# Attention in front of two dense blocks: the causal mask of the first two row tiles moves from TensorE to VectorE, one of six copies moves from ScalarE to VectorE, and the steps of a pair are written in another order

## The chip, the cores and the metric

The kernel runs on one core of a Trainium2 chip. Its time is the device time of one launch in microseconds (us), the median of several runs. TensorE (PE in the profile, PEld for its weight loads), VectorE (DVE), ScalarE (ACT) and GpSimd (POOL) each work through their own instructions in the order in which the program gives them; SyncE (SP) issues the transfers. An engine waits for another only through semaphores.

## The reference

Attention over 2 x 12 heads with 448 positions and a head size of 64, causal, in float32; then two dense blocks.

```python
scores = scale * np.matmul(q, k.transpose(0, 1, 3, 2))
mask = np.triu(np.ones((seq, seq), dtype=bool), k=1)
scores = np.where(mask, -1000000000.0, scores)
scores = scores - np.max(scores, axis=-1, keepdims=True)
attn = np.exp(scores)
attn = attn / (np.sum(attn, axis=-1, keepdims=True) + 1e-09)
attn_out = np.matmul(attn, v)
...
h = np.maximum(np.maximum(x @ w1, x @ w2), x @ w3)
x = h @ w_out
...
h = x @ w_in
r = np.maximum(h, 0.0)
out = (s * (r * r) + b) @ moe2_w_out
```

Here x has 896 rows and 768 columns.

## The kernel before

**Tiles.** Two heads make a pair; there are 12 pairs. The 448 positions of a head are four row tiles of 112, called 0 to 3, and row tile i needs the scores of the first 112 (i + 1) columns alone. `scores` (line 278) multiplies q and k for one or two row tiles of both heads into a PSUM tile `s`: six products of split operands for a row tile (line 296), the two heads in the upper and the lower half of TensorE's rows. After them come four small products of `eye` and `mask` (line 303), each 112 columns wide, which add a large negative number above the diagonal. VectorE takes the negated row maxima `mx` out of PSUM (line 312), ScalarE the exponentials into `P` with the row sums `su` (line 320). `transpose_p` (line 355) turns the 20 blocks of 112 x 112 of a pair on TensorE, in six PSUM tiles `t` (A for the first head, B for the second; 0, 1 and 2 for the column blocks 0, 1 and 2 with 3), which are copied to `PT` (line 474). `pv` (line 372) multiplies `PT` with v into the PSUM tile `o`.

**The sums.** VectorE adds 1e-9 to `su` and takes the reciprocal (steps N1 and N2, lines 478 and 481). TensorE transposes the 8 columns (RT), VectorE copies them out (RV, line 340), SyncE stores them (Q1) and spreads them over all partitions into `rb` (Q2). VectorE multiplies `o` with `rb` (XM, line 398), and GpSimd makes two parts of the result (XO, XL).

**The order.** `emit(p)` builds a table of steps by name and issues them in the order of the list `ORDER`, once for each pair; for the last two rounds, 12 and 13, by the lists in `ORDER_END`. A round p works on three pairs at once: scores, maxima and exponentials of pair p (Sb, Rb, Eb: row tile 2; Sc, Rc, Ec: row tile 3) and of pair p + 1 (Sa, Ra: row tiles 1 and 0; their exponentials Ea come in the next round), the transposes of pair p - 1 (TA0 to TB2, copies VA0 to VB2) and the products with v of pair p - 2 (P0 to P3). LD, QS, HS and LS load, scale and split q and k of later pairs: HS on VectorE, QS and LS on GpSimd. W1, W2, W3 and Y belong to the decoding of the dense blocks' weights and do something from round 10 on. `keep_busy` (line 435) issues filler products in the first rounds. There are two PSUM tiles for scores, three for transposes and one for `o`, so Sc(p) waits until Ea(p) has read Sa(p)'s tile, Sa(p + 1) until Eb(p) has read Sb(p)'s, and each group of transposes until the copy three groups before it is done.

**The dense blocks** (line 559 on) follow the last round. They are the same in both kernels.

Of the kernel before, what the change touches and what calls it, by code (L numbers as in the profile page):

```python
# [8 lines left out]
F32 = mybir.dt.float32  # L9
# [6 lines left out]
ALU = mybir.AluOpType  # L16
# [8 lines left out]


ORDER = (
    "N1 N2 TA0 Q2 LD Ea TA1 QS VA0 Sb TA2 VA1 VA2 Rb W1 HS TB0 TB1 RT Eb RV Q1 Y TB2 Sc Sa "
    "P0 Rc HS0 VB0 VB1 Ra Y VB2 P1 P2 P3 LS XM XO XL Ec"
).split()  # L30

ORDER_END = (
    "TA0 VA0 TA1 VA1 TA2 VA2 Q2 N1 N2 TB0 VB0 TB1 RT VB1 RV Q1 TB2 VB2 W1 P0 P1 P2 P3 Y Y "
    "XM XO XL W2 Y Y".split(),
    "P0 P1 P2 P3 Q2 W1 M1 M2 Y Y W2 XM XO XL M3 M4 Y Y W3 Y Y".split(),
)
# [5 lines left out]
MASKED = -(2.0 ** 30)  # L42
# [11 lines left out]
def kernel(  # L54
# [14 lines left out]
    nc = tc.nc  # L69
# [149 lines left out]
    def attention():  # L219
        with ExitStack() as c2:  # L220
            pool = lambda n, b, **kw: c2.enter_context(tc.tile_pool(name=n, bufs=b, **kw))
            mk = pool("mk", 1)
            mask, eye = (mk.tile([128, 2, CH], BF16, name=n) for n in ("mask", "eye"))
            ld = pool("ld", 4)
            vp = pool("vp", 6)
            ap = pool("ap", 3)
# [51 lines left out]
            def scores(p, tiles):  # L278

                e = pair[p]
                if "P" not in e:
                    e["P"] = p_p.tile([CH, 2, PW], F32, tag="P", name="P")
                    e["mx"] = sm.tile([CH, NC, 2], F32, tag="mx", name="mx")
                    e["su"] = sm.tile([CH, 2 * NC], F32, tag="su", name="su")
                ps = ps_s.tile([128, 2, 512], F32, tag="s", name="s")[0:CH]
                hl = [e["HL"][h * D:(h + 1) * D] for h in range(2)]
                o = 0
                offs = []  # L290
                for i in tiles:
                    n = (i + 1) * CH
                    qs = slice(i * CH, n)
                    for m, (a, c) in enumerate(((0, 2), (1, 2), (0, 3))):
                        for h in range(2):
                            nc.tensor.matmul(  # L296
                                ps[:, h, o:o + n], hl[h][:, a, qs], hl[h][:, c, 0:n],
                                start=(m == 0), stop=False, skip_group_check=True,
                            )
                    for m in range(2):  # L300
                        for h in range(2):
                            rows = slice(h * D, (h + 1) * D)
                            nc.tensor.matmul(  # L303
                                ps[:, h, o + n - CH:o + n], eye[rows, m], mask[rows, m],
                                start=False, stop=(m == 1), skip_group_check=True,
                            )
                    offs.append((i, o, n))
                    o += n

                def maxima():  # L310
                    for i, o, n in offs:
                        nc.vector.tensor_reduce(  # L312
                            out=e["mx"][:, i], in_=ps[:, :, o:o + n], op=ALU.max,
                            axis=mybir.AxisListType.X, negate=True,
                        )

                def exponentials():
                    for i, o, n in offs:
                        for h in range(2):
                            nc.scalar.activation(  # L320
                                out=e["P"][:, h, poff[i]:poff[i] + n], in_=ps[:, h, o:o + n],
                                func=ACTF.Exp, bias=e["mx"][:, i, h:h + 1], scale=1.0,
                                accum_out=e["su"][:, h * NC + i:h * NC + i + 1],
                            )

                return maxima, exponentials

            def weights_out(p, ps):

                e = pair[p]  # L330
                ps = ps[0:2 * NC, 3 * CH:4 * CH]
                rows = n_p.tile([2 * NC, CH], F32, tag="rows", name="rows")
                dram = dr_p.tile([2 * NC, CH], F32, tag="rcd", name="rcd")
                e["rb"] = n_p.tile([128, S], F32, tag="rb", name="rb")

                def transpose():
                    nc.tensor.transpose(ps, e["su"], ident[0:CH, 0:CH])  # L337

                def evacuate():
                    nc.vector.tensor_copy(out=rows, in_=ps)  # L340

                def store():
                    nc.sync.dma_start(out=dram, in_=rows)

                def spread():
                    src = dram.rearrange("(h i) n -> h (i n)", h=2)
                    for h in range(2):
                        nc.sync.dma_start(
                            out=e["rb"][h * D:(h + 1) * D],
                            in_=src[h:h + 1].to_broadcast([D, S]),  # L350
                        )

                return transpose, evacuate, store, spread
# [83 lines left out]
                    nc.tensor.matmul(ps, ones[:, 0:128], ones, start=True, stop=True)  # L437

            keep_busy(WARM)
            split_first(0)  # L440

            first = early_products(ps_s, "s")
# [2 lines left out]
            def emit(p):  # L445
                ops = {}
                if 0 <= p < n_pairs:
                    for n in "bc":
                        ops["S" + n] = lambda n=n: score[p].update(
                            {n: scores(p, (2,) if n == "b" else (3,))}  # L450
                        )
                        ops["R" + n] = lambda n=n: score[p][n][0]()
                    for n in "abc":
                        ops["E" + n] = lambda n=n: score[p][n][1]()
                    if p + 3 < n_pairs:
                        ops["LD"] = lambda: load(p + 3)
                    if p + 2 < n_pairs:
                        ops["QS"] = lambda: scale_q(p + 2)
                        ops["HS" if p else "HS0"] = lambda: split_hi(p + 2)
                        ops["LS"] = lambda: split_lo(p + 2, nc.gpsimd)  # L460
                if p + 1 < n_pairs:
                    ops["Sa"] = lambda: score[p + 1].update(a=scores(p + 1, (1, 0)))
                    ops["Ra"] = lambda: score[p + 1]["a"][0]()
                if 0 <= p - 1 < n_pairs:
                    d = {}
                    for h, k in enumerate("AB"):
                        for n, js in (("0", (0,)), ("1", (1,)), ("2", (2, 3))):
                            ops["T" + k + n] = lambda n=k + n, h=h, js=js: d.update(
                                {n: transpose_p(p - 1, h, js)}
                            )  # L470
                            copy = nc.scalar.copy
                            if p == n_pairs and n == "1":
                                copy = nc.vector.tensor_copy
                            ops["V" + k + n] = lambda n=k + n, copy=copy: copy(  # L474
                                out=d[n][0], in_=d[n][1]
                            )
                    su = pair[p - 1]["su"]
                    ops["N1"] = lambda: nc.vector.tensor_scalar(
                        out=su, in0=su, scalar1=1e-9, scalar2=None, op0=ALU.add
                    )  # L480
                    ops["N2"] = lambda: nc.vector.reciprocal(out=su, in_=su)

                    def rt():
                        pair[p - 1]["r"] = r = weights_out(p - 1, d["B1"][2])
                        r[0]()

                    ops["RT"] = rt
                    ops["RV"] = lambda: pair[p - 1]["r"][1]()
                    ops["Q1"] = lambda: pair[p - 1]["r"][2]()
                if 0 <= p - 2 < n_pairs:  # L490
                    ops["Q2"] = lambda: pair[p - 2]["r"][3]()
                    for j in range(NC):
                        ops[f"P{j}"] = lambda j=j: pv(p - 2, (j,))
                    for n, fn in zip(("XM", "XO", "XL"), pv_out(p - 2)):
                        ops[n] = fn
                if p == n_pairs + 1:
                    ops.update({f"M{n}": lambda: next(first) for n in (1, 2, 3, 4)})
                for n in CHUNKS.get(p, "").split():
                    ops[n] = begin
                ops["Y"] = lambda: finish(1)  # L500
                for n in ORDER if p < n_pairs else ORDER_END[p - n_pairs]:
                    if n in ops:
                        ops[n]()
                    if (p, n) in WARM_AT:
                        keep_busy(WARM_AT[p, n])
# [211 lines left out]
```

## Time and profile before

| what | value |
|---|---|
| median of 3 runs | 509.93 us (509.84 to 510.24) |
| the profiled execution's own time | 510.31 us |
| its span, first to last instruction | 508.5 us |
| TensorE busy over the span | 500.2 us (98%) |
| VectorE, ScalarE, GpSimd busy | 331.5, 307.1, 230.1 us |
| mean granted TensorE clock | 0.999 of full speed |

Attention takes the first 95 us of the span, the dense blocks the rest. A busy share counts the time that an engine's records cover. TensorE's records overlap, since it takes up the next product before the last has drained, so what a group of products costs is read from its own start to the start of the next group, not from the length of its records.

### The profile page before, as it was taken

How to read it: one execution, taken by the hardware profiler on the slowest of the kernel's cores; microseconds unless marked ns; L12 is line 12 of the kernel's file. 1: busy time of each engine (PE TensorE's matmuls, PEld its weight loads, DVE VectorE, ACT ScalarE, POOL GpSimd, SP SyncE). 2: the span in 40 equal slices, each digit the busy share in tenths (PEclk: the TensorE clock that was granted, in tenths of full speed). 3: DMA queues.
4: the chain of work that ended last, by engine and by line, in shares of the span. 5: the costliest groups of instructions: out<-in, count | busy, mean ns of one | idle time of the engine just before them, and what ended most of it. 6: DMA issues, size and time to landing. Idle time of an engine off the chain costs nothing.

```text
span 508.5 us, 8350 instructions
## 1 busy us (share of the span) xinstructions
PE 500.2 (98%) x3060; PEld 453.1 (89%) x3062; DVE 331.5 (65%) x642; ACT 307.1 (60%) x740; POOL 230.1 (45%) x216
## 2 busy tenths in 40 slices
PE   8899999999999999999999999999999999999997
PEld 4677777789999999999999999999999999999996
DVE  4666667787665756666666666767777985387601
ACT  4899999645453544635444888888888542354201
POOL 4556663435353443434323566666656543134300
PEclk9999999999999999999999999999999999999999
DMA  8343343433343323323332333233323352244003
GB/s 230 115 146 121 115 132 111 136 96 118 124 125 119 113 78 126 100 92 120 125 123 73 115 124 110 81 121 124 96 91 126 125 177 91 109 169 172 15 1 108
DMA packets 16185, 58.39 MB, mean 115 GB/s; under 512 B 2384, under 2 KB 6224, under 8 KB 16144
## 3 DMA queue, kind: packets, MB, share of 16 engines
q1 hardware_dynamic: 16144, 57.85, 34.5%
q8 instruction: 24, 0.39, 0.3%
q14 instruction: 17, 0.14, 0.1%
HBM read 55.05 MB, written 2.80 MB: 114 GB/s over the span
## 4 chain that ended last, share of the span: by engine, by line
PE 94%; ACT 2%; DMA 1%; DVE 1%; issue 0%; SPq 0%; POOL 0%; ACTq 0%; POOLq 0%
PE m L526 57%; PE m L647 23%; PE o L383 4%; PE t L364 4%; PE s L296 4%; ACT P L320 1%; DMA R<-in_qk_dram 1%; PE s L303 1%; PE o L526 1%; DVE mx L312 1%; ACT PT L474 0%; PE warm L437 0%; SPq L245 0%; PE t L337 0%; DVE HL L258 0%
## 5 line engine op out<-in xcount | busy, mean ns | idle before, releaser
L526 PE MATMUL m<-x,whi 128*128 128x448 f32 x804 | 228.4, 365 | 0.6 <-ACT t L535 0.6
L188 POOL TENSOR_TENSOR wa<-wa,wr 128x384 int32<-128x384 int32 x112 | 130.0, 1161 | 207.9 <-DVE wa L180 171.5
L526 PEld LDWEIGHTS m<-x,whi 128*128 128x128 f32 x804 | 150.8, 188 | 13.0 <-ACT t L535 1.0
L526 PE MATMUL m<-x,wlo 128*128 128x448 f32 x402 | 146.8, 365 | 0.0
L169 DVE TENSOR_SCALAR wa<-wa 128x384 f32<-128x384 f32 x112 | 74.4, 664 | 77.9 <-ACT wa L168 77.6
L647 PE MATMUL m<-whi,g 128*128 128x384 f32 x448 | 114.0, 334 | 0.0
L199 ACT CAST whi<-wa 128x384 fp32r<-128x384 f32 x111 | 56.4, 509 | 64.9 <-PE m L647 32.8
L647 PEld LDWEIGHTS m<-whi,g 128*128 128x128 f32 x448 | 81.0, 188 | 0.0
L526 PEld LDWEIGHTS m<-x,wlo 128*128 128x128 f32 x402 | 75.5, 188 | 6.0
L647 PE MATMUL m<-wlo,g 128*128 128x384 f32 x224 | 74.8, 334 | 0.0
L101 DVE TENSOR_TENSOR wlo<-wa,whi 128x384 fp32r<-128x384 f32 x112 | 62.2, 557 | 13.7 <-ACT whi L199 13.6
L180 DVE SCALAR_TENSOR_TENSOR wa<-wraw,wa 128x384 int32<-128x384 int32 x112 | 62.5, 558 | 3.8
L161 ACT ACTIVATE wr<-wraw 128x384 int32<-128x384 uint32 x112 | 61.5, 549 | 0.3 <-DMA wraw<-in_w_dram 0.2
L168 ACT ACTIVATE wa<-wraw 128x384 f32<-128x384 f32 x110 | 59.6, 541 | 0.0
L320 ACT ACTIVATE P<-s,mx 112x224 f32<-112x224 f32 (+3 forms) x96 | 46.3, 498 | 9.0 <-DVE mx L312 7.8
L174 DVE TENSOR_SCALAR wa<-wa 128x384 int32<-128x384 int32 x112 | 43.6, 390 | 3.8
L647 PEld LDWEIGHTS m<-wlo,g 128*128 128x128 f32 x224 | 42.0, 188 | 0.0
L526 PE MATMUL m<-h,whi 128*128 128x448 f32 x144 | 40.9, 365 | 0.0
L312 DVE TENSOR_REDUCE mx<-s 112x2 f32<-112x448 f32 (+3 forms) x48 | 33.5, 735 | 9.8 <-PE s L303 9.2
L101 POOL TENSOR_TENSOR g<-r,g 128x448 fp32r<-128x448 f32 x32 | 37.2, 1162 | 0.0
L364 PE MATMUL t<-ident,P 112*112 112x112 f32 x240 | 29.8, 264 | 1.5 <-ACT PT L474 1.5
L474 ACT COPY PT<-t 112x336 f32<-112x336 f32 (+1 forms) x70 | 29.8, 497 | 1.9 <-PE t L364 0.8
(64 smaller groups left out, 471.7 us busy)
## 6 DMA issues: line engine op xcount, KB each, us to landing
wraw<-in_w_dram SPq DMA_DIRECT2D x56, 768.0 KB
R<-in_qk_dram SPq DMA_DIRECT2D x11, 448.0 KB
V<-in_v_dram SPq DMA_DIRECT2D x12, 224.0 KB
rb<-rcd SPq DMA_DIRECT2D x24, 112.0 KB
out_dram<-o SPq DMA_DIRECT2D x14, 192.0 KB
R<-in_qk_dram SPq DMA_DIRECT2D x2, 224.0 KB
rcd<-rows SPq DMA_DIRECT2D x12, 3.5 KB
sb<-in_s_dram SPq DMA_DIRECT2D x1, 0.5 KB
```

Of the source, the lines that this page charges most:

```text
L101: eng.tensor_tensor(out=lo, in0=full, in1=hi.bitcast(F32), op=ALU.subtract)
L161: nc.scalar.activation(out=r, in_=low.bitcast(U32), func=ACTF.Copy, scale=2.0 ** -29)
L168: nc.scalar.activation(out=f, in_=fhigh, func=ACTF.Abs)
L169: nc.vector.tensor_scalar(out=f, in0=f, scalar1=UNDER, scalar2=OVER, op0=ALU.max, op1=ALU.min)
L174: nc.vector.tensor_scalar(out=a, in0=a, scalar1=3, scalar2=0x3FFFFFF8, op0=ALU.logical_shift_left, op1=ALU.bitwise_and,)
L180: nc.vector.scalar_tensor_tensor(out=a, in0=high, scalar=-0x40000000, in1=a, op0=ALU.bitwise_and, op1=ALU.bitwise_or,)
L188: nc.gpsimd.tensor_tensor(out=a, in0=a, in1=r, op=ALU.add)
L199: rest.append(lambda: nc.scalar.copy(out=hi[:, cs], in_=f))
L320: nc.scalar.activation(out=e["P"][:, h, poff[i]:poff[i] + n], in_=ps[:, h, o:o + n], func=ACTF.Exp, bias=e["mx"][:, i, h:h + 1], scale=1.0 ...
L364: nc.tensor.transpose(ps[0:CH, o:o + CH], e["P"][:, h, a:a + CH], ident[0:CH, 0:CH])
L526: nc.tensor.matmul(p, wt[w][:, ws], cols(act[i], a, b), start=(i == 0 and n == 0), stop=(i == len(act) - 1 and n == 2),)
L647: nc.tensor.matmul(acc[t][:, 0:EH], gt[f][:, a, ts], w[:, ws], start=(f == 0 and n == 0), stop=(f == KG - 1 and n == 2),)
```

## The change

The mask products (line 303) remain for row tiles 2 and 3 alone. For row tiles 0 and 1 VectorE adds a float32 tile `masks`, which GpSimd fills at the start, to the two diagonal blocks in PSUM, in one instruction ahead of Ra's two maxima. The copy VA1 goes to VectorE in every round (before, VA1 and VB1 did so in round 12 alone). N1 and N2 go: `su` is transposed as it is, RV adds the constant while it reads PSUM, and a reciprocal of the 8 x 112 result follows. RT writes into the tile of TA2, no more into that of TB1. `ORDER` is rewritten.

```diff
 ORDER = (
-    "N1 N2 TA0 Q2 LD Ea TA1 QS VA0 Sb TA2 VA1 VA2 Rb W1 HS TB0 TB1 RT Eb RV Q1 Y TB2 Sc Sa "
-    "P0 Rc HS0 VB0 VB1 Ra Y VB2 P1 P2 P3 LS XM XO XL Ec"
+    "Sb TA2 Ea TA0 RT VA2 TA1 Sc TB1 VA0 Rb RV VA1 Eb TB2 TB0 Rc QS VB1 Q1 W1 Sa Y Ra Ec HS "
+    "Q2 LD VB0 P0 P1 Y LS P2 P3 XM VB2 XO XL"
 ).split()
...
+            masks = mk.tile([CH, 2, 2, CH], F32, name="masks")
...
-                                start=(m == 0), stop=False, skip_group_check=True,
+                                start=(m == 0), stop=(i < 2 and m == 2),
+                                skip_group_check=True,
...
-                    for m in range(2):
+                    for m in range(2 if i > 1 else 0):
...
                 def maxima():
+                    if 0 in tiles:
+                        ends = ps[:, :, CH:3 * CH].rearrange("p h (i n) -> p h i n", i=2)
+                        nc.vector.tensor_tensor(out=ends, in0=ends, in1=masks, op=ALU.add)
...
-                    nc.vector.tensor_copy(out=rows, in_=ps)
+                    nc.vector.tensor_scalar(
+                        out=rows, in0=ps, scalar1=1e-9, scalar2=None, op0=ALU.add
+                    )
+                    nc.vector.reciprocal(out=rows, in_=rows)
...
+            nc.gpsimd.memset(masks, 0.0)
+            nc.gpsimd.affine_select(
+                out=masks, in_=masks, pattern=[[0, 2], [0, 2], [-1, CH]],
+                base=0, channel_multiplier=1, compare_op=ALU.is_ge, fill=MASKED,
+            )
...
-                            if p == n_pairs and n == "1":
+                            if k + n == "A1" or p == n_pairs and n == "1":
                                 copy = nc.vector.tensor_copy
...
-                    ops["N1"] = lambda: nc.vector.tensor_scalar(
-                        out=su, in0=su, scalar1=1e-9, scalar2=None, op0=ALU.add
-                    )
-                    ops["N2"] = lambda: nc.vector.reciprocal(out=su, in_=su)
...
-                        pair[p - 1]["r"] = r = weights_out(p - 1, d["B1"][2])
+                        pair[p - 1]["r"] = r = weights_out(p - 1, d["B1" if p == n_pairs else "A2"][2])
```

TensorE's program for one of the rounds 2 to 10, before (t are transposes, s scores, o products with v; a weight load of its own stands only where the operand is not the product's):

```order
L364 MATMUL t<-ident,P 112x112 x7
L296 MATMUL s<-HL 112x336 x6
L303 LDWEIGHTS eye
L303 MATMUL s<-mask,eye 112x112
...
L364 MATMUL t<-ident,P 112x112 x10
L337 MATMUL t<-ident,su 8x112
L364 MATMUL t<-ident,P 112x112 x3
L296 MATMUL s<-HL 112x448 x6
...
L296 MATMUL s<-HL 112x224 x6
...
L296 MATMUL s<-HL 112x112 x6
...
L383 MATMUL o<-PT,V 64x448 x2
```

The same round after, from the scores of row tile 2 (Sb) to the first product with v (P0):

```order
L298 MATMUL s<-HL 112x336 x6
L306 LDWEIGHTS eye
L306 MATMUL s<-mask,eye 112x112
...
L373 MATMUL t<-ident,P 112x112 x7
L343 MATMUL t<-ident,su 8x112
L373 MATMUL t<-ident,P 112x112 x3
L298 MATMUL s<-HL 112x448 x6
...
L373 MATMUL t<-ident,P 112x112 x10
L298 MATMUL s<-HL 112x224 x6
L298 MATMUL s<-HL 112x112 x6
L392 MATMUL o<-PT,V 64x448 x2
```

Before, the scores of row tiles 3, 1 and 0 stand in one stretch, each with four mask products behind it; after, ten transposes stand between row tile 3 and row tiles 1 and 0, and the latter have no mask products. A round has two stretches of scores before and three after, and two of transposes in both.

VectorE's program for such a round, before, from N1 on (mx are the maxima of Rb, and in the group of three those of Rc and Ra; HL is HS, xf is XM):

```order
L478 TENSOR_SCALAR su<-su 112x8
L481 RECIPROCAL su<-su 112x8
L312 TENSOR_REDUCE mx<-s 112x2
L258 CAST HL<-R 128x2x448
L340 COPY rows<-t 8x112
L312 TENSOR_REDUCE mx<-s 112x2 x3
L398 TENSOR_TENSOR xf<-o,rb 128x448
```

And after, from Rb on:

```order
L318 TENSOR_REDUCE mx<-s 112x2
L346 TENSOR_SCALAR rows<-t 8x112
L349 RECIPROCAL rows<-rows 8x112
L488 COPY PT<-t 112x336
L318 TENSOR_REDUCE mx<-s 112x2
L316 TENSOR_TENSOR s<-s,masks 112x2x224
L318 TENSOR_REDUCE mx<-s 112x2 x2
L259 CAST HL<-R 128x2x448
L407 TENSOR_TENSOR xf<-o,rb 128x448
```

The copy VA1 now stands ahead of Rc's maxima, the addition of the mask between Rc's and Ra's, and HS behind Ra.

## Rows read from the trace of the kernel before

**Rows 1.** Busy time of the engines in 10 us; start:end, length, engines, granted clock, transfers
```profile
core 0: us, PE busy (x) PEld busy (x) DVE busy (x) ACT busy (x) POOL busy (x), PEclk, DMA share, GB/s
50.00:60.00 10.00, 10.00 (x123) 8.07 (x123) 6.93 (x13) 9.33 (x31) 6.70 (x7) 1.00 0.46 154
```

**Rows 2.** Timeline of TensorE in round 6; start, length, engine, line, what, count
```profile
48.34 0.88 PE L364 MATMUL t<-ident,P 112*112 112x112 f32 x7
49.15 0.72 PE L296 MATMUL s<-HL 64*112 64x336 f32 x6
49.71 0.26 PE L303 MATMUL s<-mask,eye 64*112 64x112 bf16 x4
49.90 1.17 PE L364 MATMUL t<-ident,P 112*112 112x112 f32 x10
...
51.38 0.85 PE L296 MATMUL s<-HL 64*112 64x448 f32 x6
52.08 0.26 PE L303 MATMUL s<-mask,eye 64*112 64x112 bf16 x4
52.15 0.54 PE L296 MATMUL s<-HL 64*112 64x224 f32 x6
52.53 0.26 PE L303 MATMUL s<-mask,eye 64*112 64x112 bf16 x4
52.61 0.48 PE L296 MATMUL s<-HL 64*112 64x112 f32 x6
52.93 0.26 PE L303 MATMUL s<-mask,eye 64*112 64x112 bf16 x4
53.13 2.11 PE L383 MATMUL o<-PT,V 112*64 112x448 f32 x16
55.16 0.31 PE L364 MATMUL t<-ident,P 112*112 112x112 f32 x1
```

**Rows 3.** The same timeline, narrow: last two products of two groups
```profile
52.84 0.26 PE L296 MATMUL s<-HL 64*112 64x112 f32 x2
...
52.98 0.21 PE L303 MATMUL s<-mask,eye 64*112 64x112 bf16 x2
```

**Rows 4.** Groups of instructions by line and shape, first 185 us; busy us, mean ns
```profile
L303 PE MATMUL s<-mask,eye 64*112 64x112 bf16 x192 | 12.7, 209 | 0.0
L398 DVE TENSOR_TENSOR xf<-o,rb 128x448 f32<-128x448 f32 x12 | 7.5, 623 | 9.5 <-PE o L383 8.5 <-DMA rb<-rcd 0.8 <-issue 0.2
L474 DVE COPY PT<-t 112x336 f32<-112x336 f32 x2 | 1.0, 508 | 0.8 <-PE t L337 0.6 <-PE t L364 0.2
L474 ACT COPY PT<-t 112x336 f32<-112x336 f32 x46 | 19.7, 470 | 1.6 <-PE t L364 0.5
L478 DVE TENSOR_SCALAR su<-su 112x8 f32<-112x8 f32 x12 | 3.2, 269 | 0.6 <-ACT P L320 0.6
L481 DVE RECIPROCAL su<-su 112x8 f32<-112x8 f32 x12 | 2.4, 203 | 0.4
```

**Rows 5.** Timeline of TensorE in rounds 1 to 3
```profile
18.15 0.54 PE L296 MATMUL s<-HL 64*112 64x224 f32 x6
...
22.84 0.88 PE L364 MATMUL t<-ident,P 112*112 112x112 f32 x7 [0.70 <-ACT PT L474]
...
27.84 0.88 PE L364 MATMUL t<-ident,P 112*112 112x112 f32 x7
```

**Rows 6.** Timeline of ScalarE in round 2
```profile
20.73 0.44 ACT L320 ACTIVATE P<-s,mx 112x224 f32<-112x224 f32 x1
...
22.23 1.23 ACT L474 COPY PT<-t 112x448 f32<-112x448 f32 x3
```

**Rows 7.** Timeline of VectorE: both maxima of a Ra
```profile
13.06 0.92 DVE L312 TENSOR_REDUCE mx<-s 112x2 f32<-112x448 f32 x2
```

**Rows 8.** Timeline of TensorE: where rounds 10 and 11 start
```profile
75.64 0.88 PE L364 MATMUL t<-ident,P 112*112 112x112 f32 x7
...
82.80 0.88 PE L364 MATMUL t<-ident,P 112*112 112x112 f32 x7
```

**Rows 9.** Timeline of the weight loads in round 10
```profile
79.76 0.37 PEld L296 LDWEIGHTS s<-HL 64*112 64x112 f32 x6 [0.25 <-ACT P L320]
```

More of the change, by code (lines that the diff above doesn't have):

```diff
@@ L27 @@
 ORDER = (
-    "N1 N2 TA0 Q2 LD Ea TA1 QS VA0 Sb TA2 VA1 VA2 Rb W1 HS TB0 TB1 RT Eb RV Q1 Y TB2 Sc Sa "
-    "P0 Rc HS0 VB0 VB1 Ra Y VB2 P1 P2 P3 LS XM XO XL Ec"
+    "Sb TA2 Ea TA0 RT VA2 TA1 Sc TB1 VA0 Rb RV VA1 Eb TB2 TB0 Rc QS VB1 Q1 W1 Sa Y Ra Ec HS "
+    "Q2 LD VB0 P0 P1 Y LS P2 P3 XM VB2 XO XL"
 ).split()
 ORDER_END = (
-    "TA0 VA0 TA1 VA1 TA2 VA2 Q2 N1 N2 TB0 VB0 TB1 RT VB1 RV Q1 TB2 VB2 W1 P0 P1 P2 P3 Y Y "
+    "TA0 VA0 TA1 VA1 TA2 VA2 Q2 TB0 VB0 TB1 RT VB1 RV Q1 TB2 VB2 W1 P0 P1 P2 P3 Y Y "
     "XM XO XL W2 Y Y".split(),
@@ L458, in emit @@
                         ops["QS"] = lambda: scale_q(p + 2)
-                        ops["HS" if p else "HS0"] = lambda: split_hi(p + 2)
+                        ops["HS"] = lambda: split_hi(p + 2)
                         ops["LS"] = lambda: split_lo(p + 2, nc.gpsimd)
@@ L476, in emit @@
                             )
-                    su = pair[p - 1]["su"]
-                    ops["N1"] = lambda: nc.vector.tensor_scalar(
-                        out=su, in0=su, scalar1=1e-9, scalar2=None, op0=ALU.add
-                    )
-                    ops["N2"] = lambda: nc.vector.reciprocal(out=su, in_=su)
                     def rt():
-                        pair[p - 1]["r"] = r = weights_out(p - 1, d["B1"][2])
+                        pair[p - 1]["r"] = r = weights_out(p - 1, d["B1" if p == n_pairs else "A2"][2])
                         r[0]()
```

## The prediction

> **What bounds the kernel now.** I read first the table of busy times by stretch. In the middle of the attention [rows 1] TensorE is covered for all of 10.00 us at the full clock, ScalarE for 9.33, VectorE for 6.93. Then the timeline of TensorE alone over one round, by its starts [rows 2]. Round 6 begins with seven transposes at 48.34 and round 7 at 55.16, so a round takes 6.82 us, and no row of it carries an idle note: TensorE waits for nobody, and the round is the sum of its groups, each from its start to the next one's. Transposes 0.81; row tile 2's scores 0.56 and mask 0.19; 14 transposes (the sums' one among them) 1.48; row tile 3's scores 0.70, mask 0.07; row tile 1's 0.38, mask 0.08; row tile 0's 0.32, mask 0.20; products with v 2.03. Work taken off ScalarE and VectorE is therefore worth nothing in a round, and the change is to be priced on TensorE: what the missing mask products save, and what the new order of groups costs.
>
> **TensorE's groups, in two kinds of place.** The same four mask products take 0.07 and 0.08 where more scores follow, and 0.19 and 0.20 where transposes or products with v follow [rows 2]. The extra 0.12 is a price for changing the form of the products. The narrow rows show it a second way: the last two mask products start at 52.98, 0.05 behind the two before them (52.93), and the next form only 0.15 later, at 53.13 [rows 2, 3]. Transposes have it too: 14 take 1.48 and 7 take 0.81, so one takes 0.096 and a group has a fixed 0.14. Scores right behind another form take 0.56 (336 columns) and 0.70 (448), a step of 0.14 for 112 columns; by that line row tile 1's 224 columns would take 0.42 there, against 0.38 behind other scores.
>
> The Trainium skill, TensorEngine Tiling (Array Packing), Tiling Modes, says that going from one tiling of the array to another drains TensorE. These rows agree, with 0.12 a change (scores use 64 rows a head, transposes 112). By that rule the change gives back part of what it saves, since it makes such changes more frequent; a reader who prices the mask products alone would expect about three times my gain.
>
> **A round after.** Sa, the scores of row tiles 1 and 0, took 0.38 + 0.08 + 0.32 + 0.20 = 0.98. Now they follow transposes and have no masks: 0.42 + 0.32, and the way out to the products with v. That way was 0.10 from the last two scores (52.84) to the mask, and would be 0.15 straight to another form: 0.05 more. Together 0.79, a saving of 0.19. Against it, row tile 3's mask is now followed by transposes: 0.19 in place of 0.07, a loss of 0.12. The 21 transposes are in two groups as before (11 and 10), 2.29 either way; a round now goes from products with v to scores in place of transposes, which I price the same. Net 6.82 - 0.19 + 0.12 = 6.75, or 0.07 a round. From both sides: if nothing but the four-and-four mask starts went and the order were free, 0.28; the eight products at their busy time of 12.7 / 192 = 0.066 each give 0.53 [rows 4]. If the way out of Sa cost the whole 0.12 on top, Sa would take 0.86 and the round 6.82, no gain; with 0.05 more for products with v followed by scores, 0.05 lost. I take 0.07, the sum of the nearest rows. Rounds 3 to 9: 7 x 0.07 = 0.5.
>
> **Does TensorE still bound the round?** VectorE gains the addition, 448 elements a partition with one operand in PSUM: nearest row XM, 0.62. It writes to PSUM, which no row shows; bounds 0.51 (the copy of 336 out of PSUM) and twice XM, 1.25. VA1 adds 0.51. N1 and N2 go (0.27 and 0.20), the reciprocal of 112 columns comes in at some 0.2 [rows 4]. From 6.93 in 10 us, 4.7 a round, it goes to about 5.6 of 6.75. ScalarE loses a copy of 0.47 [rows 4]. What queues: the addition stands between Rc and Ra, behind it HS, XM and the next Rb. Counted from the start of Sb, the groups of TensorE add up: Sb 0.75, 11 transposes 1.20, so Sc starts at 1.95; with 0.89 and 1.10 Sa starts at 3.94, and at 4.73 the products with v. So Sa has drained at 4.8, the addition at 5.5, Ra at 6.4; Ea then runs to 1.3 of the next round, and Sc, which needs its tile, comes at 1.95. So 0.6 is spare: an addition up to 1.2 costs nothing in a round. HS ends at 7.0, LS on GpSimd at 9.1, 1.6 ahead of Sa in the next round (3.9); XM is done at 7.6, before the next Rb needs VectorE. VA1 (2.2 to 2.7) frees the tile for TB0 at 3.4. On SyncE's queue Q2 and LD now stand behind Q1, which waits for RV at 2.2; `rb` is not read before 6.9. RV's reciprocal lies on this path alone. GpSimd's two instructions for `masks` run while it would wait for the first loads. All of this is covered, at a cost of nothing; if the cover of 0.6 were gone, each further 0.1 of the addition would cost 0.1 a round.
>
> **The start.** In rounds 1 and 2 TensorE does wait. The seven transposes of round 2 at 22.84 waited 0.70 for copies behind Ea [rows 5]. There the addition is on the path (scores, addition, maxima, Ea, Sc). I put Sa(2) at 18.1 as before (18.15): the first two Ea come 0.4 later (0.62 less the masks' 0.2), but the transposes of round 1 no longer hold up Sc. Its scores end at 18.1 + 0.79 + 0.15 = 19.04, the addition with hand-overs at 19.75, Ra (0.92 [rows 7]) at 20.7. Ea(2), which began at 20.73 and handed over at 22.23 [rows 6], thus runs at nearly its old time, to 22.2. Sc then at 22.25, 0.70 + 0.19 to 23.14; ten transposes 1.10, 24.24; Sa 0.79, 25.03; products with v 2.03, 27.06. Before, that point was 27.84 [rows 5]: 0.75 gained. Bounds: an addition at 1.25 costs 0.6 in each of three rounds, a loss of about 1; if Sa(2) starts 0.6 earlier, a gain of 1.35.
>
> **The end.** Round 10 took 82.80 - 75.64 = 7.16 [rows 8], 0.34 more than a round, 0.25 of it as Sa's weight load waited for ScalarE [rows 9], where decoding (W1) stood ahead of Eb. Now W1 stands behind Eb on ScalarE and behind Rc on VectorE, where three instructions of it delay Ra by about 0.3, within the 0.6: 0.33 + 0.07 = 0.4 gained. Bounds 0 and 0.4. Round 11 has no Sa and the same changes of form: nothing. In round 12 the order differs by N1 and N2 alone: nothing, within 0.3 either way.
>
> **Sum.** 0.5 + 0.75 + 0.4 = 1.65. The profiled execution took 510.31 (span 508.5 and 1.8 around it), which gives 508.66; the median of the runs is 0.38 below it, so 508.3.
>
> **Rivals.**
> - The order is free. Nothing is lost by changing form and each of 12 pairs saves the mean of 0.28 and 0.53, 0.40: 4.8 us, 505.1. For it: no row shows products with v followed by scores. Against it: the 0.12 shows at two places of every round. 0.10.
> - The gain of the start and of round 10 isn't there, because Ea, Eb and Sc wait in turn from the start on with the addition among them, and a round gains 0.07 or less: 0 to 0.9, some 509.5. For it: ScalarE is at 93% and rounds 1 and 2 wait for it. Against it: it loses a copy. 0.23.
> - Slower: one more change of form a round costs more than Sa saves. It decides from 0.19 on: the 0.12 shown, the 0.04 of the cold start of Sa, and 0.12 (not 0.05) on Sa's way out leave nothing, and at 0.1 more for scores behind products with v a round takes 6.92. Over 8 rounds 0.8 lost, and at the start the addition three times with little of the masks back, 1.1: 511.8. For it: each piece is near its row. Against it: a narrow row puts Sa's way out at 0.05. 0.13.
> - The forecast, gains of 1.0 to 3.3 us: 0.54, own range 506.6 to 509.0.
>
> A difference under 0.2%, 1.0 us, can't be told from none here. Faster 0.54 + 0.10 and a little less for gains just under 1 us: 0.62. Same 0.24, slower 0.14. The range reaches towards both far rivals and leaves out the larger half of each, 0.12 in all: 505.6 to 510.8.
>
> **What will show it.** The starts of the products with v in rounds 5 and 6 lie 6.75 apart (6.43 for the first rival, over 6.82 for the third). No mask products between 224 and 112 columns; row tile 3's mask takes 0.19 to the transposes. The addition has a mean near 0.62. Round 3's first scores start near 27.1, round 10 is no longer than the others, and the dense blocks' own length stays. I am wrong if TensorE shows idle notes in rounds 4 to 9, if the addition is over 1.2, or if the span of the dense blocks moves by more than 0.5.

## The result and the profile after

| | before | after |
|---|---|---|
| median | 509.97 us (509.66 to 510.24, 6 runs) | 513.49 us (513.24 to 513.87, 6 runs) |
| span of the profiled execution | 508.5 us | 511.6 us |
| rounds 3 to 9, first P to first P | 7 x 6.83 | 5 x 7.15, 7.36, 7.43 |
| first product of the dense blocks | 95.27 | 98.16 |

The change makes the kernel slower: ratio 1.007, 95% interval 1.0059 to 1.0081. The forecast was 508.3, and the time lies outside its range (505.6 to 510.8). Four launches, one of the kernel before, two of e10 and one of e12, took 618 to 2804 us and are left out of the times and intervals. By the starts of the first product with v (P) in each round the 3.1 us of span divide so: up to round 2's P 0.27 gained, rounds 3 to 9 2.74 lost, round 10 nothing, round 11 0.45 lost (6.42 for 5.97), rounds 12 and 13 0.03 gained, dense blocks 0.21 lost.

The 10 us of [rows 1] again, columns as there, after the change:

```profile
50.00:60.00 10.00, 9.57 (x96) 7.17 (x94) 8.52 (x15) 8.35 (x31) 6.85 (x7) 1.00 0.45 130
```

The clock is the same. TensorE, covered without a gap before, now has gaps, VectorE went from 6.93 to 8.52, ScalarE from 9.33 to 8.35. Where the gaps are, the timeline of TensorE in round 4 shows (against [rows 2]):

```profile
36.67 0.88 PE L298 MATMUL s<-HL 64*112 64x448 f32 x6
37.38 0.26 PE L306 MATMUL s<-mask,eye 64*112 64x112 bf16 x4
37.58 0.79 PE L373 MATMUL t<-ident,P 112*112 112x112 f32 x6
38.57 0.59 PE L373 MATMUL t<-ident,P 112*112 112x112 f32 x4 [0.20 <-DVE PT L488]
39.09 0.82 PE L298 MATMUL s<-HL 64*112 64x224 f32 x12
39.84 2.11 PE L392 MATMUL o<-PT,V 112*64 112x448 f32 x16
41.88 0.71 PE L298 MATMUL s<-HL 64*112 64x336 f32 x6
```

Sc's mask takes 0.20 to the transposes (forecast 0.19), Sa 0.75 (0.79), P 2.04 (2.03). But the ten transposes in the middle break after six and take 1.51, not 1.10: the last four, TB0, wait for a VectorE copy, VA1. 7.15 less this 0.41 is 6.74; forecast were 6.75. Rounds 10 and 11 break at the same place, and their ten transposes take 1.54 and 1.49; in round 11:

```profile
88.16 0.79 PE L373 MATMUL t<-ident,P 112*112 112x112 f32 x6
89.12 0.60 PE L373 MATMUL t<-ident,P 112*112 112x112 f32 x4 [0.18 <-DVE PT L488]
```

VectorE in round 4:

```profile
37.02 0.26 DVE L346 TENSOR_SCALAR rows<-t 8x112 f32<-8x112 f32 x1 [0.30 <-ACT PT L488]
37.31 0.84 DVE L349 RECIPROCAL rows<-rows 8x112 f32<-8x112 f32 x1
38.08 0.43 DVE L488 COPY PT<-t 112x336 f32<-112x336 f32 x1
38.44 1.06 DVE L318 TENSOR_REDUCE mx<-s 112x2 f32<-112x896 f32 x1
40.02 0.63 DVE L316 TENSOR_TENSOR s<-s,masks 112x448 f32<-112x448 f32 x1 [0.52 <-PE s L298]
...
42.38 0.62 DVE L407 TENSOR_TENSOR xf<-o,rb 128x448 f32<-128x448 f32 x1 [0.23 <-DMA rb<-rcd]
```

RV waits for ScalarE's copy VA2, its reciprocal takes 0.84, and only then VA1 comes, ending at 38.51, just before TB0 starts at 38.57. The last row is a second wait: XM for `rb`. Groups by shape over the first 185 us (against [rows 4]; busy us, mean ns) show that these lengths are the rule:

```profile
L349 DVE RECIPROCAL rows<-rows 8x112 f32<-8x112 f32 x12 | 10.1, 841 | 0.4
L316 DVE TENSOR_TENSOR s<-s,masks 112x448 f32<-112x448 f32 x12 | 7.6, 631 | 5.1 <-PE s L298 5.1
```

The waits from 20 to 95 us (us in total, times, longest):

```profile
PEld t L373 <- DVE PT L488: 4.7, 10, 0.7
DVE rows L346 <- ACT PT L488: 3.9, 9, 0.9
DVE xf L407 <- DMA rb<-rcd: 3.8, 7, 1.0
```

In the kernel before, XM waits once for `rb` in this stretch (0.8, in round 12), and TensorE never for a VectorE copy.

### The profile page after: what moved, and what is told of

It reads as the page before. It is cut to its first block, busy times and chain, and to the rows that moved or that the text cites. A ratio compares the mean times of both kernels' runs of the same rounds, so it can differ in the third digit from the quotient of the medians.

```text
span 511.6 us, 8194 instructions
## 1 busy us (share of the span) xinstructions
PE 500.3 (98%) x2964; PEld 450.3 (88%) x2966; DVE 346.4 (68%) x653; ACT 304.4 (59%) x729; POOL 232.4 (45%) x218
## 4 chain that ended last, share of the span: by engine, by line
PE 90%; DVE 5%; ACT 3%; DMA 1%; issue 1%; SPq 0%; ACTq 0%; DVEq 0%
PE m L534 56%; PE m L655 23%; PE o L392 4%; PE t L373 3%; PE s L298 2%; DVE rows L349 2%; ACT P L326 2%; ACT PT L488 1%; DVE mx L318 1%; DVE PT L488 1%; DMA R<-in_qk_dram 1%; PE o L534 1%; DVE rows L346 1%; DVE s L316 0%; PE t L343 0%
## 5 line engine op out<-in xcount | busy, mean ns | idle before, releaser
L169 DVE TENSOR_SCALAR wa<-wa 128x384 f32<-128x384 f32 x112 | 73.0, 651 | 77.8 <-ACT wa L168 77.6
L174 DVE TENSOR_SCALAR wa<-wa 128x384 int32<-128x384 int32 x112 | 44.9, 401 | 3.8
L101 POOL TENSOR_TENSOR HL<-R,HL 128x896 fp32r<-128x896 f32 x11 | 23.1, 2096 | 31.4 <-DVE HL L259 27.2
L373 PE MATMUL t<-ident,P 112*112 112x112 f32 x240 | 31.7, 266 | 2.8 <-DVE PT L488 2.7
```

Source lines behind the costliest of these rows:

```text
L101: eng.tensor_tensor(out=lo, in0=full, in1=hi.bitcast(F32), op=ALU.subtract)
L169: nc.vector.tensor_scalar(out=f, in0=f, scalar1=UNDER, scalar2=OVER, op0=ALU.max, op1=ALU.min)
L174: nc.vector.tensor_scalar(out=a, in0=a, scalar1=3, scalar2=0x3FFFFFF8, op0=ALU.logical_shift_left, op1=ALU.bitwise_and,)
L373: nc.tensor.transpose(ps[0:CH, o:o + CH], e["P"][:, h, a:a + CH], ident[0:CH, 0:CH])
```

## The experiments

Theories at the outset: R, the 0.84 of the reciprocal ahead of VA1 holds TB0. Q, the place of VA1 behind RV (and RV's wait for VA2) is enough for that, however short RV's work is. M, the addition and the new changes of form are themselves the cost. Ratios are to the kernel before, with 95% intervals. Diffs of the order show only the piece of `ORDER` that differs.

**e1_early_reciprocal.** The reciprocal back on the 112x8 sums, early.
```diff
-Sb TA2
+N1 N2 Sb TA2
```


> The changed kernel with one part undone: 1e-9 is added and the reciprocal taken on the sums as they lie (112 rows x 8), first in a round, and RV is a plain copy again. Theory R (the reciprocal of 8 x 112 takes 0.84 us ahead of VA1 and so holds TB0): no idle note at TB0, a round of 6.75, some 508.5 us. Theory Q (VA1 waits for its place behind RV, whatever RV does, and RV waits for VA2): half of the 0.41 at TB0 stays, a round of 6.95, 510.5. Theory M (the addition of the mask and the added changes of form are what costs): 512 to 513.

519.19, ratio 1.0187 (1.0172 to 1.0202): far slower, in rounds of 8.05. VectorE, then GpSimd, in round 5:

```profile
44.26 1.81 DVE L488 TENSOR_SCALAR su<-su 112x8 f32<-112x8 f32 x1
46.10 0.20 DVE L491 RECIPROCAL su<-su 112x8 f32<-112x8 f32 x1
```
```profile
43.96 2.08 POOL L100 TENSOR_TENSOR HL<-R,HL 128x896 fp32r<-128x896 f32 x1 [3.67 <-DVE HL L258]
```

The reciprocal of 8 elements a partition takes 0.20. But N1, which took 0.16 at its place in most rounds before, takes 1.81 and ends at 46.07, 0.03 after GpSimd's LS (46.04). The sums' transpose waits 1.18 for them. The ten transposes in the middle run without a break here, but the kernel says little about R (508.5 expected), since it put a new wait in. The Trainium skill, SBUF — State Buffer, SBUF: two separate sides, says that VectorE, in a mode that uses two ports or with two inputs in SBUF, and GpSimd share a pair of ports, which the first to start holds for its whole instruction. N1's end with LS fits that; no run shows which mode N1 ran in.

**e2_copy_first.** VA1 ahead of RV.
```diff
-Rb RV VA1 Eb
+Rb VA1 RV Eb
```


> The changed kernel with two steps exchanged: VA1 stands ahead of RV on VectorE, the reciprocal of 8 x 112 stays. R and Q alike: TB0 no longer waits, a round of 6.75 unless Rc, which now starts at 3.8 behind the reciprocal, sends Ec and Ea late: 508.5 to 509.5 us. M: 512 to 513.

513.32 (1.0055 to 1.0089). The first rounds take 6.72, 6.71 and 6.73, with no wait of TensorE for VA1, so that wait was 0.43 a round. Then the second wait takes over, in a round of 8.32 (VectorE, then TensorE):

```profile
57.34 0.62 DVE L406 TENSOR_TENSOR xf<-o,rb 128x448 f32<-128x448 f32 x1 [2.51 <-DMA rb<-rcd]
57.88 0.85 DVE L317 TENSOR_REDUCE mx<-s 112x2 f32<-112x672 f32 x1
58.65 0.50 DVE L487 COPY PT<-t 112x336 f32<-112x336 f32 x1
```
```profile
59.20 0.89 PE L372 MATMUL t<-ident,P 112*112 112x112 f32 x7 [1.25 <-DVE PT L487]
```

XM stands 2.51 for `rb`; Rb and VA1 queue behind it on VectorE, and the last seven of the ten transposes wait for VA1 again. R and Q had expected 508.5 to 509.5 here: wrong, since they did not count Q2, which stands behind Q1 and so behind the reciprocal, now later still. The time alone would fit M (512 to 513) nearly; the first rounds don't.

**e3_copy_on_scalar.** VA1 back on ScalarE.
```diff
-if k + n == "A1" or p == n_pairs and n == "1":
+if p == n_pairs and n == "1":
```


> The changed kernel with VA1 back on ScalarE, at the same place in the list, everything else as changed. R and Q: TB0 waits for ScalarE, which is free by 2.5 in a round; a round of 6.75 to 6.85, 508.5 to 509.5 us. M: 512 to 513. If ScalarE's 0.35 more is what counts (ScalarE binds), 514 or more.

511.21 (1.0018 to 1.0086; two of ten launches at 516.6 and 517.3 widen the interval), all rounds 6.92, for 6.75 to 6.85 expected. TB0 waits no more, and Sa's weight load waits 0.34 to 0.36 for Eb on ScalarE in rounds 3 to 10, which costs 0.2 a round beside the 6.72 of e2. So taking the sixth copy off ScalarE was right, and its place was not.

**e4_masks_on_tensor.** The mask products of row tiles 0 and 1 back, no addition.
```diff
-for m in range(2 if i > 1 else 0):
+for m in range(2):
...
-    nc.vector.tensor_tensor(out=ends, in0=ends, in1=masks, op=ALU.add)
```


> The changed kernel with the masks of row tiles 0 and 1 back on TensorE and no addition on VectorE. R and Q: the wait at TB0 stays and Sa is 0.19 to 0.23 longer, a round of 7.35, 515.5 us. M: the addition was the cost, so 510 to 512.

515.10 (1.0092 to 1.0122), rounds of 7.40 but two (8.01 and 8.11), as R and Q had it (7.35, 515.5). In the new order the moved mask gains 0.25 a round, so the addition is not the cost, and half of M falls. The other half, the changes of form, falls with the rounds of 6.72 in e2 and e6, which keep the addition and all changes of form.

**e5_spread_first and e6_copy_and_spread_first.** Q2 to the front of the round; in e6 VA1 ahead of RV as well.
```diff
-Sb TA2
+Q2 Sb TA2
...
-HS Q2 LD
+HS LD
```


> The changed kernel with one step moved: Q2, the spreading of the reciprocals of pair p - 2 into `rb`, is issued first in a round, ahead of Q1, which waits for the reciprocal of pair p - 1; nothing else is touched. Theory R (the 8x112 reciprocal of 0.84 holds VA1 and by it TB0) with the late `rb` as a second, smaller term: the two long rounds (7.36 and 7.43) become 7.15 like the others, XM waits for no DMA, and 0.5 us goes: 513.0. Theory Q (the place of VA1 behind RV counts, whatever RV does): the same 513.0 by the same term. Rival: the late `rb` is the main term, since it blocks Rb behind XM on VectorE in every round: rounds of 6.8, 510.5.

> The changed kernel with two steps moved: VA1 stands ahead of RV on VectorE and Q2 first in the round. With VA1 first alone, three rounds took 6.72 and the later ones up to 8.32, with XM waiting for `rb`. Theory R and the late `rb` as two separate terms: rounds of 6.72 all through, M (the first product of the dense blocks) near 94.9, 509.8 less what the start gives, so 509.0 to 510.0. Rival: what lengthened the later rounds is the 0.84 of the reciprocal on VectorE itself, which delays Rc, the addition and Ra wherever it stands: rounds of 7.0 and more remain, 512 or above.

e5: 513.99 (1.0063 to 1.0093). XM's waits for `rb` are gone in attention, one of the two long rounds becomes 7.15, the other stays at 7.45; round 11 takes 6.95. No gain by itself, while TB0 waits (R and Q had expected 513.0). e6: 510.00 (0.9992 to 1.0011), rounds of 6.72 but one (6.90). So either step moved alone leaves the time about where it was (513.3 and 514.0), and both together give 3.5 us: in e5 the wait for VA1 still sets the round, and in e2 the wait for `rb`, which the exchange made longer, takes its place. Still the time is only that of before, and round 11 takes 6.93 (before 5.97). VectorE in round 10, and TensorE in round 11:

```profile
78.87 1.06 DVE L163 TENSOR_SCALAR wa<-wraw 128x384 int32<-128x384 int32 x1
79.96 0.36 DVE L168 TENSOR_SCALAR wa<-wa 128x384 f32<-128x384 f32 x1
80.36 0.36 DVE L173 TENSOR_SCALAR wa<-wa 128x384 int32<-128x384 int32 x1
80.64 0.63 DVE L315 TENSOR_TENSOR s<-s,masks 112x448 f32<-112x448 f32 x1
```
```profile
84.03 0.86 PE L297 MATMUL s<-HL 64*112 64x448 f32 x6 [0.89 <-ACT P L325]
```

Decoding (W1) stands in round 10 ahead of the addition; that, Ra and Ea come late, and Sc of round 11 waits 0.89.

**e7_masks_alone and e8_sums_alone.** One part each in the kernel before, with its old order: the addition (diff as in the change), or the sums' new form.
```diff
-nc.vector.tensor_copy(out=rows, in_=ps)
+nc.vector.tensor_scalar(out=rows, in0=ps, scalar1=1e-9, scalar2=None, op0=ALU.add)
+nc.vector.reciprocal(out=rows, in_=rows)
```


> The kernel before with one part of the change: the masks of row tiles 0 and 1 are added by VectorE ahead of Ra's maxima; order, sums and copies stay as they were. Theory R (the addition is cheap, the sums' new form is the loss): 8 mask products go, a round takes 6.5 to 6.6 (0.28 less, and Ra 0.6 later is covered by the spare time before Ea), 507.0 to 508.0. Rival: the addition delays Ra and with it Ea, which stands early on ScalarE in the old order, and Sc by it: rounds of 6.8 or longer, 510 to 512.

> The kernel before with another part alone: `su` is transposed as it is, RV adds the constant out of PSUM and takes the reciprocal of the 8x112 result; masks stay on TensorE, copies on ScalarE, the order is the old one without N1 and N2. Theory R: the reciprocal takes 0.84 here too (mean of L481's successor), but in the old order RV stands behind Rb and HS with no copy behind it, so that Rc alone is held: rounds of 6.8 to 7.0, 509.9 to 511.5. Theory Q (VA1's place decides, not the reciprocal's length): no change, rounds of 6.82, 510.0. Rival: N1 and N2 were on the path at the start of a round (they wait for Ec), and leaving them out gains: 508.5.

e7: 512.44 (1.0032 to 1.0062), rounds of 7.03, against my expectation (507.0 to 508.0); the rival had the rounds (6.8 or longer), and 510 to 512. e8: 512.55 (1.0034 to 1.0064), rounds of 6.83 and 7.34 in turn, worse than R gave (6.8 to 7.0). TensorE of e7, then of e8:

```profile
44.83 0.88 PE L369 MATMUL t<-ident,P 112*112 112x112 f32 x7 [0.23 <-ACT PT L484]
```
```profile
51.02 0.88 PE L367 MATMUL t<-ident,P 112*112 112x112 f32 x7 [0.29 <-ACT PT L477]
```

Both wait at the same place, for copies that queue on ScalarE behind exponentials, whose maxima come late: counted from the start of the products with v, Ra ends after 1.17 in the kernel before, 2.09 in e7 (its addition takes 0.62) and 1.84 in e8 (its reciprocal takes 0.84). In the old order there is no room for either; in the new one there is for the addition (rounds of 6.72 in e6).

**e9_no_reciprocal.** The kernel after, with RV's reciprocal left out.
```diff
-nc.vector.reciprocal(out=rows, in_=rows)
```


> The changed kernel without the reciprocal of the 8x112 rows: RV only adds the constant, so the output is multiplied by the sums in place of being divided. Everything else, the order and the waits of RV and VA1 among it, is untouched. Theory R (the 0.84 of the reciprocal ahead of VA1 is what holds TB0, and its store what makes `rb` late): the 0.41 of waiting in a round goes, rounds of 6.75, no wait of XM for `rb`, 508.7 to 509.2. Theory Q (the place of VA1 behind RV, and RV behind VA2, is enough): TB0 still waits 0.2 or more, rounds of 6.95 to 7.15, 511 to 513.

TensorE, then VectorE, in round 4:

```profile
36.87 1.17 PE L372 MATMUL t<-ident,P 112*112 112x112 f32 x10
37.97 0.81 PE L298 MATMUL s<-HL 64*112 64x224 f32 x12
38.72 2.11 PE L391 MATMUL o<-PT,V 112*64 112x448 f32 x16
```
```profile
36.33 0.26 DVE L346 TENSOR_SCALAR rows<-t 8x112 f32<-8x112 f32 x1 [0.57 <-ACT PT L487]
36.52 0.48 DVE L487 COPY PT<-t 112x336 f32<-112x336 f32 x1
```

Ten transposes in one go, rounds of 6.71 to 6.73 but one (6.87), though RV still waits for VA2 and VA1 still stands behind RV. R holds and Q falls. But the time is 509.57 (0.9984 to 1.0003), above R's 508.7 to 509.2. Attention ends 1.16 earlier than before (94.11), and the dense blocks take 414.52 in place of 413.22. From 20 us on XM waits for `rb` only twice, 0.17 once and 2.87 in round 12; e13 takes that wait up.

**e10_decoding_later.** e6 with W1 behind Ra.
```diff
-Q1 W1 Sa Y Ra Ec
+Q1 Sa Ra W1 Y Ec
```


> The changed kernel with VA1 ahead of RV, Q2 first, and W1 with its Y behind Ra in place of between Rc and Ra. With the first two alone (510.0) rounds took 6.72 but Sc of round 11 waited 0.89 for Ea, as decoding stood ahead of the addition and Ra on VectorE. If that is the term: round 11 falls from 6.93 to about 6.0 and the time by 0.9, to 509.1. Rival: the decoding that comes later makes the dense blocks start later, and the same 0.9 comes back in round 12 or in the first dense products: 510.0.

Round 11 takes 6.00, as expected, and the dense blocks start at 94.15. But the time is 509.83 (0.9989 to 1.0009), above the 509.1 expected and near the rival's 510.0: of the 0.93, round 12 takes back 0.31 and the dense part (413.78) 0.11. The trace's span is 0.52 shorter than e6's, the median 0.17; the rest is spread of runs.

**e11_sums_ahead.** e10 with the reciprocal at 112x8, between Ra and HS, the 1e-9 left out, and RV a plain copy.
```diff
-Sa Ra W1 Y Ec HS
+Sa Ra Ec N2 W1 Y HS
```


> As the kernel with decoding later, and the reciprocal back on the 112x8 sums (8 elements a partition), at the end of the pair's own round, between Ra and HS, where GpSimd is idle by the trace (before LS); the constant 1e-9 is left out, as float32 rounds it away beside sums that are at least 1; RV is a plain copy again. If the reciprocal's length goes by the elements of a partition it takes 0.2 there, and the late `rb` of the last pair (0.44 more in the first dense products) goes: 508.5 to 508.7. Rival: N2 waits for Ec on ScalarE and pushes HS, LS and XM back, rounds of 6.8 and more, 509.5 or above.

The reciprocal takes 0.19 (mean of 12) and delays nobody, rounds are 6.72; yet 509.93 (0.9991 to 1.0010), not 508.5 to 508.7, the dense blocks at 413.89. Missed: the last pair's own reciprocal was not what they wait for.

**e12_fewer_changes.** Four changes of form in a round.
```diff
-Sb TA2 Ea TA0 ... TA1 Sc TB1 ... TB2 TB0 ... Sa
+Sc TA2 TA0 Ea VA2 TA1 TB1 VA0 TB0 Rc VA1 TB2 RT Ec RV Y QS HS Sb ... Sa
```


> A new order with four changes of form in a round on TensorE in place of six: Sc, then all 20 transposes and the sums' one, then Sb and Sa next to each other, then the products with v; the masks of tiles 0 and 1 on VectorE, one copy on VectorE, sums as in the kernel with the sums ahead. By 0.11 a change a round takes 6.72 - 0.22 = 6.5, and the time comes to 506.5 to 507.0, if nobody is waited for. Rival: ScalarE has 6.2 us of work in such a round with two chains that leave under 0.2 (Ec before Sa, Eb before the next Sc), and TensorE waits for it: rounds of 6.7 to 6.9, 508.5 to 510.

510.05 (0.9996 to 1.0015), not 506.5 to 507.0, rounds of 6.69. The groups add up to 6.54, but after 13 transposes a weight load waits 0.15 for a ScalarE copy behind Ea, each round, and round 2's P comes 0.8 later than in e11. The rival was right about who waits.

**e13_spread_ahead_of_weights and e14_before_spread_ahead.** One transfer earlier, in e10 and in the kernel before: pair 10's reciprocals are spread in round 11 (Q3).
```diff
-ops["Q2"] = lambda: pair[p - 2]["r"][3]()
+if p != n_pairs:
+    ops["Q2"] = lambda: pair[p - 2]["r"][3]()
...
+if p == n_pairs - 1:
+    ops["Q3"] = lambda: pair[p - 1]["r"][3]()
```


> The kernel with decoding later, and one transfer moved: the spreading of pair 10's reciprocals is issued in round 11, right behind their store, and so ahead of a 768 KB load of weights; before and after it is issued in round 12 behind that load. Theory S (the forecast's gain goes lost at the end of attention: VectorE stands 0.8 to 2.9 us in XM of pair 10 for `rb` that lands behind the weights, with the decoding of the dense blocks queued behind XM): the wait of 1.5 goes, the dense blocks take 413.2 in place of 413.8, 509.3 to 509.5 in place of 510.0. Rival D (the dense blocks have a due time of their own, the weights' loads and decoding): the wait moves elsewhere and the time stays at 510.0.

> The kernel before with that one transfer moved likewise. Theory S: its wait of XM for `rb` is 0.84, TensorE loses little by it there (the dense blocks take 413.2), so 509.5 to 510.0, at most 0.4 gained. Rival D: no change at all, 510.0, though the wait of XM is gone.

Issues on SyncE's queue in e10 and XM of pair 10 on VectorE, then the same in e13:

```profile
88.48 0.36 SPq L143 DMA_DIRECT2D wraw<-in_w_dram  x1
89.03 1.09 SPq L356 DMA_DIRECT2D rb<-rcd  x2
```
```profile
94.83 0.62 DVE L406 TENSOR_TENSOR xf<-o,rb 128x448 f32<-128x448 f32 x1 [1.47 <-DMA rb<-rcd]
```
```profile
86.64 1.08 SPq L356 DMA_DIRECT2D rb<-rcd  x2
88.63 0.37 SPq L143 DMA_DIRECT2D wraw<-in_w_dram  x1
```
```profile
93.42 0.61 DVE L406 TENSOR_TENSOR xf<-o,rb 128x448 f32<-128x448 f32 x1
```

e13: 509.15 (0.9978 to 0.9996), dense part 413.23. e14: 510.00 (0.9990 to 1.0009), dense part 413.21. The intervals of e10 and e13 overlap a little, so the traces decide: S holds. In e10 XM starts 5.8 us after the issue of its `rb` began; in the kernel after, in the rounds that wait for `rb`, it is 3.6 to 4.5. Behind XM come, on VectorE, the decoding and the last pair's x, and in the first dense products of e10 weight loads of TensorE wait 0.17 for the decoding's `wlo`, and 0.17 and 0.47 for x. In e13 none of these waits is left. What is not shown is whether the load ahead of `rb` counts or only the time of its issue, since e13 moves it ahead of the load and 2.4 us earlier in one. In the kernel before, the wait is 0.84 and covered: the dense part is as long with it as without.

**e15_two_orders and e16_fewer_changes_2.** The four-change order with N2 behind XM and Q3; e15 with e11's order in the rounds before round 2.
```diff
-for n in ORDER if p < n_pairs else
+for n in ORDER_START if p < 2 else ORDER if p < n_pairs else
```


> The order with four changes of form from round 2 on, N2 moved behind XM so that Ea does not stand behind it (it took 0.15 from TensorE in each round), the order of the kernel with the sums ahead in the first rounds (P of round 2 at 25.3 in place of 26.0), and pair 10's spreading ahead of the weights. If the terms add up: rounds of 6.55, 0.7 less at the start, and a dense part of 413.2: 507.0 to 508.0. Rival D: the dense blocks wait for their weights and take 414 or more, 509.5.

> As the kernel with two orders, with the new order in the first rounds too. If the start counts as its trace says, 0.7 above the kernel with two orders: 507.7 to 508.7. Rival D: the same time as that one, 509.5, since the dense blocks' own due time decides.

e15: 508.97 (0.9976 to 0.9993), 0.16% under before, the lowest median, though not told apart from e13; 507.0 to 508.0 were expected. e16: 509.70 (0.9989 to 1.0008), for 507.7 to 508.7. Dense part 413.22 in both, so rival D falls; the sums fell short as the rounds did not get shorter. TensorE in round 6 of e15, then the weight load that waits:

```profile
47.54 0.86 PE L301 MATMUL s<-HL 64*112 64x448 f32 x6
48.24 0.26 PE L309 MATMUL s<-mask,eye 64*112 64x112 bf16 x4
48.44 2.39 PE L373 MATMUL t<-ident,P 112*112 112x112 f32 x20
...
50.85 0.72 PE L301 MATMUL s<-HL 64*112 64x336 f32 x6
```
```profile
49.94 0.67 PEld L373 LDWEIGHTS t<-ident,P 112*112 112x112 f32 x7 [0.16 <-ACT PT L491]
```

Rounds stay at 6.69, not 6.55: moving N2 did not help, as Ea waits for Ra and the copies for Ea. The two medians differ by 0.73, near the 0.7 expected of the start. The one trace of each has 1.78 (round 2's P at 25.40 and 27.18), and that of e16 is of a launch 1.0 above its median.

## Why the prediction was wrong

- **"the reciprocal of 112 columns comes in at some 0.2 [rows 4]"**: this step failed. The row it was read from has 8 elements a partition; the new instruction has 112, and takes 0.84. The same 896 elements cost four times as much on 8 partitions as on 112, so the cost goes with the elements in a partition; if it is linear between these two shapes, (841 - 203) ns / 104 = 6.1 ns an element, an estimate. The Trainium skill, VectorE: DVE Perf Modes, First, the fixed hardware budget, says that reciprocal runs as an iterated division; 0.84 beside 0.26 for the addition on the same 8x112 fits that, and no run shows the iteration.
- **"VA1 (2.2 to 2.7) frees the tile for TB0 at 3.4"** and **"RV's reciprocal lies on this path alone"** fell with it. From Sb's start (34.73) VA1 ends at 3.78, TB0 starts at 3.84. The second was wrong in itself: on VectorE, VA1 and Rc queue behind the reciprocal. I listed what queues for the addition and not for the reciprocal. What the runs showed in place of a cover "at a cost of nothing" is a wait of TB0 for VA1 of 0.43 a round, and with it the idle notes of TensorE that the prediction named as its sign of being wrong. Shown by e9 and by e2's first rounds: 0.43 a round, 7 x 0.43 = 3.0; with 0.49 for the two long rounds, less 0.2 for the round's 6.72 in place of 6.75, that is the 2.74 + 0.5 missed in rounds 3 to 9, the larger part of the 5.2 us between 508.3 and 513.49. Rounds 10 and 11 missed some 0.4 each by the same wait.
- **"`rb` is not read before 6.9 ... covered"** failed too. I counted Q2 behind RV but not the 0.84 in RV. XM waits 0.2 to 1.0 in 7 places; that costs little while TB0 waits longer (e5 takes one of the two long rounds away), and with VA1 ahead of RV, which makes `rb` later still, it cost about as much (e2).
- **A round of 6.75** without the wait was right: 6.72 in e2, e6, e9 and e10. So were the pieces: Sc's mask 0.20, Sa 0.75, the addition 0.63, and its 0.6 of spare time (in e6 Ea ends at 75.68, 0.66 ahead of Sc).
- **The start, 0.75 gained** (0.78 by its own figures, 27.84 less 27.06): measured 0.27. It can't be told from one profile: the kernel before and e14, alike up to there, reach round 2's P at 25.80 and 25.12.
- **Round 10, 0.4 gained**: it is no longer than the others, as forecast, but at 7.15 for 7.16 nothing was gained, since the wait for VA1 took the 0.4; without it e6 has 6.73. "Round 11 ... nothing" failed by the same wait (6.42 for 5.97). And "three instructions of it delay Ra by about 0.3" was too little: in the kernel after they take 1.06 and the addition comes 0.46 later behind Rc than in round 4, at next to no cost. In e6, where TB0 no longer waits, they take 1.8, and Sc of round 11 waits 0.89; e10 gives back 0.93.
- **"the dense blocks' own length stays"**: within 0.21 in the kernel after. In the faster kernels it did not stay (413.66 to 414.52) until the transfer moved. So even with the reciprocal's length right, 508.3 would have been too low, by 1.3 as far as e9 (509.57) shows and by 0.8 as far as e13 (509.15) does.
- The rival for slower gave 511.8 by another mechanism, changes of form; these cost what was forecast. Slower came from none of the causes I had listed.

What stays open: the one round of 6.87 to 6.92 among 6.72 in e6, e9, e10, e11 and e13, and what moves the start by 0.7 from one execution to the next. In e6's long round ScalarE's copies start behind the transposes that follow the sums' one, 0.58 idle in place of 0.30, and a weight load of TB1 waits 0.23 for them; why that round alone does so isn't shown.

## What to carry to other kernels

Read the price of an operation from a row with the same elements per partition, not the same count of elements: here a transposed operand had four times the price. When an instruction grows on an in-order engine, list what queues behind it, even if its own result is not urgent; and where two waits hide each other, taking one away shows nothing, so remove them together before giving a theory up. A gain in one stage shows only if the next stage is ready for it: look for what that stage waits for that has not moved.

## What the runs showed of the hardware

A reciprocal took 0.20 us on 112 partitions of 8 elements and 0.84 on 8 partitions of 112. A TENSOR_SCALAR of 8 elements a partition on VectorE took 1.81 us beside a 2.08 us instruction of GpSimd (e1), and 0.16 without; the kernel after, which adds the constant out of PSUM, takes 0.25 to 0.26 for it in all rounds. The addition into PSUM took as long as XM's multiplication out of it (0.63 and 0.62, both of 448 elements a partition).
